# One order of work exchanged for another behind the first batch of a fused attention and feed-forward kernel, with three gates on batch 2's loads

## The chip, the cores and the metric

The kernel runs on one core of a Trainium2 chip. The metric is the device time of one execution in microseconds (us); lower is better. A core has five engines that run their own instruction streams side by side: TensorE (PE) for matrix products, VectorE (DVE), ScalarE (ACT) and GpSimd (POOL) for elementwise work, and SyncE (SP), which here only issues DMA transfers. Each stream runs in order: an instruction that waits holds up everything behind it on its engine.

## What is computed

Linear attention over 8 batches of 8 heads, 576 positions and 64 dimensions, then a feed-forward part with a product of two branches:

```python
q_s = softmax(q, over the head dimension)
k_s = softmax(k, over the positions)
kv = np.einsum('bhsd,bhse->bhde', k_s, v)
x = np.einsum('bhsd,bhde->bhse', q_s, kv)   # then to (4608 tokens, 512)
a = x @ w1                                   # 512 x 1024
b = x @ w2
h = a * b @ w3                               # 1024 x 1024
out = h @ w_out                              # 1024 x 512
```

## The kernel before

The work is cut into steps. Every step has a name, an engine, and the steps that it needs; a table written out by hand, `ORDER`, lists all 977 of them, and `Plan.run` emits them in that order. So the place of a step in the list sets its place in its engine's stream, and a suffix (/A, /D, /P) picks ACT, DVE or POOL where there is a choice. Waits between engines follow from the data and the buffers. Steps marked as `port` on DVE and POOL also wait for the one listed ahead of them on the other of the two.

The number behind a step's name is its batch (0 to 7) or its chunk of 512 tokens (0 to 7, and chunk 8 for the tails of all batches). The steps that matter here, with their lines:

- `q.b`, `k.b`, `v.b`, `w1.i`, `w2.i`: loads (line 354). The weights and batches 0 and 1 are issued from POOL, but for q of batch 0; batches 2 to 7 from SP. `w1.1` is the second half of the columns of w1, 512 KB after its cast to 16 bits; a batch's q, k or v is 1152 KB. q, k and v have two buffers each, used in turn.
- `qmx`, `qsub`, `qexp`, `qsm`, `qeps`, `qrc`, `qn`: softmax of q in two parts per batch: row maximum (DVE, L529), subtraction (L535), exponential (ACT, L543), row sum (DVE, L561), reciprocal (DVE, L572), product (L579). `qd` (SP, L613) turns the result by a DMA transpose.
- `kmx`, `cb`, `ksub`, `kexp`: the same for k over positions: column maximum (DVE, L427), its spread over the partitions (DVE, L451 to L462), subtraction (L466), exponential (ACT, L474). `vc` casts v (L271).
- `kv` (PE, L492) sums k_s times v, `kv2` (DVE, L510 to L513) divides by the sums, `xm` and `xt` (PE, L631) give x, `xs` and `xts` (ACT mostly, L275) copy it out of PSUM.
- `up.1.c.s.u` and `up.0.c.s.u` (PE, L787): x times a block of columns of w2 and of w1; `bs` (ACT, L271) copies the first out, `ab` (DVE, L802) multiplies the two. Chunks 0 and 1 do it in two halves of tokens, s = 0 and 1, with u from 0 to 3; blocks u = 2 and 3 use `w1.1` and `w2.2`.
- `down` (PE, L809) multiplies by w3 @ w_out, which is folded once at the start; `os` copies out, `st` (SP, L836) stores.
- Chunks 5 to 8 form their products by Strassen's scheme with seven products in place of eight: `xd`, `ws`, `um`, `ue`, `uc` going up, and for chunks 4 to 7 `ad`, `wt`, `dm`, `de`, `dc` coming down.

PSUM has eight banks, taken by the PE steps in the listed order and freed by the copies that read them. So a late `ab` holds up the PE step that takes its bank next.

A gate makes a load wait for another load. Before, the first load on SP behind the two early ones (it is `q.2`) waits for the third-last load on POOL (it is `w1.1`); behind `w1.1` POOL issues `q.1.1` and `v.1`:

```python
gate = gates.get(name)
if gate:
    tc.add_manual_dep(st[name].ins, st[gate].ins.name, ..., reason="load order")
...
loads = [n for n in listed if plan.steps.get(n, {}).get("kind") == "load"]
gates[[n for n in loads if plan.steps[n]["eng"] == "SP" and n not in EARLY][0]] = [
    n for n in loads if plan.steps[n]["eng"] == "POOL"][-GATE]
```

Of the kernel before, what the change touches and what calls it, by code (L numbers as in the profile page):

```python
# [121 lines left out]
qsm.6.1 qeps.6.1/A ab.4.0.5 ksub.6.0/P xt.4 xts.4.0/A xts.4.1/A ksub.6.1/P kexp.6.0 qsm.6.0 st.0.3 kv.5 qeps.6.0/A
kv2.5 bs.4.0.6/A qrc.6.0 qn.6.0/P qrc.6.1 down.3.0 os.2.3/A down.3.1 kexp.6.1 qd.5.1 xm.5.0 os.3.0/A xs.5.0.0/A
qmx.7.0 xs.5.0.1/A os.3.1/A qmx.7.1 xm.5.1 xs.5.1.1/A xs.5.1.0/A up.0.4.0.6 up.1.4.0.7 um.5.0.1 ue.5.0.1/A ws.2.1/D
ws.3.0/D um.5.1.1 vc.6.0/A ue.5.1.1/A k.7 wt.4/D ad.4.3/D down.3.2 os.3.2/A xd.5.3/D um.5.1.7 xd.5.1/D xd.5.2/D
ws.4.1/D xd.5.4/D um.5.1.6 um.5.0.6 qn.6.1/P ue.5.1.2/A ue.5.0.2/A ab.4.0.4 ab.4.0.6 um.5.0.7 qd.6.0 ue.5.0.7/A
up.0.4.0.7 um.5.0.2 ue.5.1.7/A bs.4.0.7/A qd.6.1 um.5.1.2 kmx.7.0 qsub.7.1/P qexp.7.1 uc.5.1.1 um.5.0.4 qsub.7.0/P
uc.5.0.3 um.5.0.5 um.5.1.4 ab.4.0.7 down.3.3 uc.5.1.3 os.3.3/A ue.5.0.4/D xt.5 xts.5.1/D ab.5.1.0/P qexp.7.0 xts.5.0/A
kv.6 um.5.1.5 uc.5.0.1 ab.5.0.0/P ue.5.1.4/A uc.5.0.4/P um.5.3.1 ue.5.3.1/A um.5.2.7 kv2.6 ue.5.2.7/A qsm.7.1 xm.6.1
xs.6.1.0/A xm.6.0 st.2.3 um.5.0.3 um.5.3.6 um.5.1.3 um.5.2.1 xs.6.0.1/A xs.6.1.1/D uc.5.1.4/D um.5.3.7 st.3.0  # L130
ue.5.3.2/A um.5.3.5 ad.4.1/D qeps.7.1/A qrc.7.1 ad.4.2/D um.5.2.2 ue.5.2.1/A um.5.2.6 xs.6.0.0/A xd.6.3/P um.5.3.2 v.7
uc.5.2.1 ab.5.1.1 ue.5.3.7/A um.5.3.4 uc.5.3.3 ue.5.3.4/A um.5.2.4 uc.5.3.4/P xd.6.2/P um.6.1.1 ue.5.2.2/A uc.5.2.3
ab.5.2.0/P qsm.7.0 ue.6.1.1/A um.5.2.5 dm.4.7 de.4.7/A ab.5.0.1 uc.5.3.1 qeps.7.0/D dm.4.1 de.4.1/A xd.6.1/D um.6.1.6
ad.4.4/D ue.5.2.4/A qrc.7.0 uc.5.2.4/P um.5.3.3 xt.6 ab.5.3.1 xts.6.1/D um.6.1.7 dm.4.6 dm.4.4 xts.6.0/A xd.6.4/P
kmx.7.1 dm.4.2 um.6.1.2 ue.6.1.2/A dc.4.1 um.5.2.3 vc.7.1/A ab.5.2.1 ue.6.1.7/A um.6.1.4 ab.5.3.0/P de.4.2/A um.6.2.7
st.2.0 uc.6.1.3 st.3.1 qn.7.0/P um.6.1.5 ue.6.1.4/A uc.6.1.4/P dm.4.5 dc.4.3 uc.6.1.1 de.4.4/A um.6.3.7 cb.7 dc.4.4/P
ue.6.2.7/A um.6.0.1 ue.6.3.7/A ue.6.0.1/A ab.6.1.0/D um.6.0.7 ue.6.0.7/A dm.4.3 dc.4.2/A ad.5.3/D um.6.3.1 ksub.7.0/D
ue.6.3.1/A um.6.2.1 ue.6.2.1/A um.6.2.4 ksub.7.1/D um.6.1.3 um.6.3.6 um.6.3.4 dm.5.7 ue.6.3.2/A uc.6.3.3 vc.7.0/A
um.6.2.6 ue.6.2.2/A qn.7.1/P uc.6.2.3 um.6.0.6 ue.6.0.2/A um.6.3.5 ue.6.3.4/D kexp.7.0 um.6.0.4 um.6.2.5 um.6.3.2
uc.6.0.3 uc.6.3.1 um.6.2.2 uc.6.2.1 ab.6.1.1 uc.6.3.4/P um.6.0.5 ue.6.0.4/A uc.6.0.4/P um.6.3.3 ab.6.3.1 dm.5.2  # L140
ad.5.1/D um.6.0.3 dm.5.1 kexp.7.1 kv.7 qd.7.0 ad.5.2/D kv2.7 de.5.7/A ue.6.2.4/A de.5.1/A dm.5.4 dm.5.6 de.5.2/A
ab.6.3.0/P st.4.1 um.6.2.3 dc.5.1 ab.6.0.1 uc.6.2.4/P qd.7.1 xm.7.1 xs.7.1.0/D xm.7.0 ad.5.4/D xs.7.1.1/A dm.5.5
um.7.0.2 xs.7.0.1/A xs.7.0.0/A xd.7.1/D de.5.4/A xd.7.3/D xd.7.2/D st.4.0 xt.7 xd.7.4/P xts.7.1/A xts.7.0/A um.6.0.2
um.7.1.1 dc.5.3 dm.5.3 uc.6.0.1 um.7.0.1 dc.5.2/D ue.7.1.1/A dc.5.4/P ue.7.0.1/A um.7.1.6 ue.7.1.2/D um.7.0.7 um.7.1.2
uc.7.1.1 ab.6.0.0/P ue.7.0.7/A um.7.1.7 ue.7.1.7/A um.7.0.6 ue.7.0.2/A uc.7.0.1 um.7.1.5 um.7.2.1 ab.6.2.1 ue.7.2.1/A
ab.6.2.0/D um.7.3.1 um.7.2.2 uc.7.2.1 um.7.0.5 um.7.1.4 ue.7.1.4/A um.7.0.4 uc.7.1.3 um.7.1.3 uc.7.0.3 st.5.0 um.7.3.2
dm.6.1 um.7.2.6 ue.7.0.4/A ad.6.1/P ad.6.2/D um.7.3.7 uc.7.0.4/D ue.7.3.1/A um.7.3.6 uc.7.3.1 uc.7.1.4/D um.7.2.7
um.7.0.3 ab.7.0.0/D ab.7.1.1 ue.7.2.2/A ad.6.3/D ab.7.1.0/P de.6.1/D ue.7.3.7/A ab.7.0.1 dm.6.2 um.7.2.5 ue.7.3.2/A
um.7.3.5 ue.7.2.7/A dc.6.1 um.7.3.4 dm.6.7 de.6.7/A xd.8.3/P st.5.1 uc.7.3.3 um.7.2.4 uc.7.2.3 dm.6.6 st.3.2
ue.7.2.4/A ue.7.3.4/A uc.7.3.4/D uc.7.2.4/D de.6.2/A xd.8.1/D ad.6.4/D xd.8.2/D dm.6.4 um.8.3.7 um.7.2.3 ue.8.3.7/A  # L150
# [975 lines left out]
```

## Time and profile before

| | |
|---|---|
| time, median of 3 runs | 233.28 us (233.26 to 234.73) |
| the profiled execution: its time, its span | 233.08 us, 231.3 us |
| PE busy | 220.6 us, 95% of the span |
| DVE, ACT, POOL busy | 205.2, 154.0, 155.4 us |
| PE's mean granted clock | 0.997 of full speed |
| moved by DMA | 46.88 MB, mean 203 GB/s |

The profile is one execution, recorded by the hardware. Its span runs from the first to the last instruction; the time of an execution also holds a little around it. A row of a group of instructions gives the line, the engine, the operation, output <- input with shapes, the count, busy time, the mean of one in ns, and the idle time of the engine ahead of them with what ended it. A row in order of time gives start, duration and, in brackets, idle time ahead and its releaser. "SPq" and "POOLq" rows are issues of DMA transfers; a transfer lands some microseconds after its issue.

### The profile page before, as it was taken

To read this page: it belongs to the slowest core of one execution; us is meant where nothing else is said; L and a number is where in the kernel's file an instruction comes from. 1 tells how busy PE (TensorE), PEld (TensorE's weight loads), DVE (VectorE), ACT (ScalarE), POOL (GpSimd) and SP (SyncE) were. 2 spreads that over 40 slices of the span, in tenths; PEclk is the share of its full clock that TensorE was granted. 3 is DMA by queue.
4 is the path that set the end of the run, shared out by engine and by line. 5 is a ranking of instruction groups with operands and counts; after the bars stand their busy time and mean duration, and the time that the engine had idled before them with its cause. 6 is when DMAs were issued, how large, how long until landed. Compare 5 with 4: busy or idle time off the path is not lost.

```text
span 231.3 us, 5574 instructions
## 1 busy us (share of the span) xinstructions
PE 220.6 (95%) x2226; PEld 148.3 (64%) x2226; DVE 205.2 (89%) x346; ACT 154.0 (67%) x254; POOL 155.4 (67%) x105
## 2 busy tenths in 40 slices
...
GB/s 221 215 285 233 308 230 237 388 348 328 203 372 206 350 402 211 270 260 363 265 198 81 294 36 240 150 286 12 12 127 108 44 159 71 4 111 116 3 214 148
DMA packets 38105, 46.88 MB, mean 203 GB/s; under 512 B 18112, under 2 KB 21568, under 8 KB 38080
## 3 DMA queue, kind: packets, MB, share of 16 engines
...
## 4 chain that ended last, share of the span: by engine, by line
PE 72%; DMA 12%; DVE 12%; issue 1%; POOL 1%; ACT 0%; ACTq 0%; POOLq 0%; DVEq 0%
PE pab L787 21%; PE uA L871 12%; DMA w<-in_moe_w_dram 9%; PE po L809 8%; PE dA L911 6%; PE uB L871 6%; DVE km L427 5%; DMA k<-in_k_dram 4%; PE pf L396 3%; PE uC L871 3%; PE dB L911 3%; PE po L824 3%; DVE ab L802 2%; PE pkv L492 2%; PE xm L631 2%; PE dC L911 2%
## 5 line engine op out<-in xcount | busy, mean ns | idle before, releaser
L787 PE MATMUL pab<-x,w2sb 128*128 128x256 f16 (+1 forms) x224 | 40.4, 318 | 0.8 <-ACT x L275 0.8
L787 PE MATMUL pab<-x,w1sb 128*128 128x256 f16 (+1 forms) x224 | 40.2, 318 | 1.0 <-DVE ab L802 1.0
L466 POOL TENSOR_TENSOR k<-k,cb 128x1152 f32<-128x1152 f32 x11 | 28.7, 2629 | 11.8 <-DVE q L535 10.7
L579 POOL TENSOR_TENSOR en<-eq,qr 128x1024 f16<-128x1024 f16 (+1 forms) x14 | 29.7, 2124 | 9.7 <-DVE v L850 4.6
L427 DVE TENSOR_REDUCE km<-k 128x128 f32<-128x1152 f32 x14 | 30.5, 2188 | 3.2 <-DMA k<-in_k_dram 3.2
L787 PEld LDWEIGHTS <-w2sb 128*128 128x128 f16 x224 | 21.5, 98 | 14.6 <-issue 2.2
L787 PEld LDWEIGHTS <-w1sb 128*128 128x128 f16 x224 | 21.8, 98 | 13.9 <-issue 1.6
L809 PE MATMUL po<-W3O,ab 128*128 128x512 f16 x128 | 29.4, 379 | 0.1
L535 POOL TENSOR_TENSOR q<-q,qm 128x1280 f32<-128x1280 f32 (+1 forms) x13 | 27.6, 2143 | 1.0 <-DVE qm L529 1.0
L271 ACT CAST bsb<-pab 128x512 f16<-128x512 f32 x40 | 23.0, 592 | 7.0 <-PE pab L787 6.3
L871 PEld LDWEIGHTS <-w 128*128 128x128 f16 x256 | 24.8, 98 | 3.6 <-issue 0.4
L543 ACT ACTIVATE eq<-q 128x1024 f16<-128x1024 f32 (+2 forms) x16 | 18.7, 1180 | 12.0 <-DVE q L535 9.0
L802 DVE TENSOR_TENSOR ab<-pab,bsb 128x512 f16<-128x512 f32 x40 | 25.7, 670 | 0.1
L529 DVE TENSOR_REDUCE qm<-q 128x16 f32<-128x1024 f32 (+2 forms) x16 | 21.1, 1330 | 4.0 <-DMA q<-in_q_dram 4.0
L561 DVE TENSOR_REDUCE qr<-eq 128x16 f32<-128x1024 f16 (+2 forms) x16 | 21.4, 1338 | 0.0
L809 PEld LDWEIGHTS <-ab 128*128 128x128 f16 x128 | 12.3, 98 | 13.6
L275 ACT ACTIVATE x<-xm 128x512 f16<-128x512 f32 x30 | 16.1, 606 | 6.8 <-PE xm L631 5.9
L474 ACT ACTIVATE ek<-k 128x1152 f16<-128x1152 f32 x16 | 18.4, 1167 | 2.8 <-POOL k L466 2.8
L271 ACT COPY q<-uA 128x512 f32<-128x512 f32 x22 | 13.0, 594 | 8.7 <-PE uA L871 6.9
L871 PE MATMUL uA<-v,w 128*128 128x256 f16 x128 | 18.4, 273 | 0.0
L271 ACT COPY outs<-po 128x512 f32<-128x512 f32 (+1 forms) x19 | 10.7, 568 | 9.2 <-PE po L824 4.5
L396 PE MATMUL pf<-wosb,aux 128*128 128x512 f16 x64 | 15.6, 379 | 0.5 <-DMA wosb<-in_moe_w_out_dram 0.5
...
## 6 DMA issues: line engine op xcount, KB each, us to landing
q<-in_q_dram SPq DMA_DIRECT2D x6, 1152.0 KB, 7.2
k<-in_k_dram SPq DMA_DIRECT2D x6, 1152.0 KB, 9.4
v<-in_v_dram SPq DMA_DIRECT2D x6, 1152.0 KB, 8.1
...
```

Source lines behind the costliest of these rows:

```text
L271: return [(nc.scalar.copy if eng == "ACT" else engine[eng].tensor_copy)(out=out, in_=in_)]
L396: nc.tensor.matmul(st["pf", ft], lhsT=st["w3T", ft][:, gt, :], rhs=wosb[:, gt, :], start=(gt == 0), stop=(gt == N_FT - 1))
L427: dve.tensor_reduce(out=st["km", b][:, two(hp), :], in_=kb[:, two(hp), :, :].rearrange("p h j d -> p h d j"), axis=AX.X, op=ALU.max)
L466: return [engine[eng].tensor_tensor(out=kb[:, two(hp), :, :], in0=kb[:, two(hp), :, :], in1=st["cb", b][:, two(hp), None, :].broadcast_to( ...
L535: return [engine[eng].tensor_tensor(out=qb[:, hs, j, :], in0=qb[:, hs, j, :], in1=st["qm", b][:, hs, j, None].broadcast_to([P, nh, n, D]), ...
L561: dve.tensor_reduce(out=st["qr", b][(slice(None), *part(p))], in_=st["eq", b, p], axis=AX.X, op=ALU.add)
L579: return [engine[eng].tensor_tensor(out=st["en", b][:, j, hs, :].rearrange("p j h d -> p h j d"), in0=st["eq", b, p], in1=st["qr", b][:, h ...
L787: nc.tensor.matmul(st["p", one, c, sub, u][:, a * (t1 - t0):(a + 1) * (t1 - t0)], lhsT=w[:, ct, fb * P:(fb + 1) * P], rhs=x()[:, ct, t0:t1 ...
L802: dve.tensor_tensor(out=st["ab", c][:, nf * u:nf * u + nf, t0:t1], in0=cut(st["p", 0, c, sub, u]), in1=cut(st["bsb", c, sub, u]), op=ALU.mult)
L809: nc.tensor.matmul(st["po", c, tb], lhsT=st["ab", c][:, ft, tb * P:(tb + 1) * P], rhs=W3O[:, ft, :], start=(ft == 0), stop=(ft == N_FT - 1))
L871: nc.tensor.matmul(t[:, u, :], lhsT=w[:, k0 + kk, fb * P:(fb + 1) * P], rhs=r[:, kk, :], start=(p in (1, 2, 7) and u == 0 and kk == 0), st ...
L911: nc.tensor.matmul(t[:, i, :], lhsT=l[:, f, i * P:(i + 1) * P], rhs=r[:, f, :], start=(p in (1, 2, 7) and i == 0 and f == 0), stop=(i == 1 ...
```

## The change

`GATE` and the code that chose the gated load go; a table names the three gated loads and `w1.1` for each of them. `ORDER` is another list of the same 977 steps, equal in the first 140; 56 of the steps that may run on one of two engines run on the other one. Behind `w2.2`, POOL issues `v.1`, `q.1.1`, `w1.1`. Steps, buffers and tiles stay as they are.

```diff
-GATE = 3
+GATES = {(n, 2): ("w1", 1) for n in "qkv"}
...
-up.1.0.1.2 bs.0.1.2/A up.1.0.0.2 up.1.0.0.3 ab.0.0.1 qsm.1.0 qeps.1.0/A qrc.1.0 bs.0.0.3/A bs.0.0.2/A kexp.1.1
-bs.0.1.3/A w1.1 up.0.0.1.2 q.1.1 qmx.1.1 v.1 ksub.1.0/P kexp.1.0 vc.1.1/A up.0.0.0.2 up.0.0.1.3 qn.1.0/P up.0.0.0.3
-ab.0.0.2 ab.0.1.2 ab.0.0.3 down.0.0 down.0.1 ab.0.1.3 q.2 qmx.2.0 qsub.1.1/P qexp.1.1 qsm.1.1 vc.1.0/P kv.1.0 kv.1
-kv2.1 os.0.0/A os.0.1/A qeps.1.1/A qrc.1.1 qmx.2.1 qsub.2.0/P qexp.2.0 qsm.2.0 down.0.2 down.0.3 os.0.2/A k.2 qd.1.0
-q.3 kmx.2.0 v.2 xm.1.0 xs.1.0.0/A xs.1.0.1/A os.0.3/A xt.0 xts.0.1/A ws.1.0/P up.1.1.0.0 up.0.1.0.0 kmx.2.1 up.1.1.0.1
-up.0.1.0.1 qn.1.1/P qd.1.1 bs.1.0.0/A ab.1.0.0 qsub.2.1/P qeps.2.0/A qrc.2.0 qexp.2.1 vc.2.1/A bs.1.0.1/A q.4
-up.1.1.0.2 up.0.1.0.2 xts.0.0/A xm.1.1 xs.1.1.1/A wt.1/P k.3 st.0.0 cb.2 qn.2.0/P qd.2.0 bs.1.0.2/A qsm.2.1 xt.1
-up.1.1.0.3 ab.1.0.1 up.0.1.0.3 ksub.2.1/P xs.1.1.0/A up.1.1.1.0 qeps.2.1/A bs.1.0.3/A xts.1.1/A kexp.2.1 bs.1.1.0/A
-qrc.2.1 qn.2.1/P qd.2.1 qmx.3.1 up.0.1.1.0 up.1.1.1.1 up.0.1.1.1 vc.2.0/A bs.1.1.1/A ab.1.0.3 ksub.2.0/P st.0.2
-ab.1.0.2 qmx.4.0 qmx.3.0 kexp.2.0 kmx.3.0 down.1.0 qmx.4.1 down.1.1 os.1.1/A os.1.0/A kv.2 v.4 up.1.1.1.2 up.0.1.1.2
-xts.1.0/A bs.1.1.2/A kv2.2 xm.2.0 xs.2.0.0/A xs.2.0.1/A xm.2.1 xs.2.1.0/A v.3 kmx.3.1 st.1.0 cb.3 xs.2.1.1/A
-qsub.3.0/P up.1.1.1.3 up.0.1.1.3 up.1.2.0.0 bs.1.1.3/A qsub.3.1/P ab.1.1.3 qexp.3.1 qsm.3.1 k.4 bs.2.0.0/A up.0.2.0.0
-up.1.2.0.1 up.0.2.0.1 qsub.4.1/P qexp.4.1 up.1.2.0.2 up.0.2.0.2 ab.2.0.0 qexp.3.0 q.5 bs.2.0.1/A qeps.3.1/A ab.1.1.0
-qsub.4.0/P qsm.3.0 ksub.3.1/P ksub.3.0/P qrc.3.1 qexp.4.0 ab.1.1.1 up.1.2.0.3 up.0.2.0.3 bs.2.0.3/A ab.1.1.2 qsm.4.1
-up.1.2.0.4 up.0.2.0.4 up.1.2.0.5 qn.3.1/P qeps.3.0/A qrc.3.0 vc.3.1/A kmx.4.0 bs.2.0.4/A ab.2.0.4 down.1.2 qn.3.0/P
-up.0.2.0.5 bs.2.0.2/A kexp.3.0 kexp.3.1 vc.3.0/A kv.3 ab.2.0.1 ws.2.0/P bs.2.0.5/A os.1.2/A qmx.5.0 wt.3/P qd.3.1
-qeps.4.1/A qrc.4.1 qsub.5.0/P xt.2 xts.2.0/A ab.2.0.5 xts.2.1/A down.1.3 os.1.3/A up.1.2.0.6 ab.2.0.2 up.0.2.0.6
-qd.3.0 kv2.3 xm.3.1 xs.3.1.1/A q.6 qn.4.1/P ws.4.0/P xm.3.0 st.1.3 xs.3.0.0/A xs.3.0.1/A kmx.4.1 cb.4 xs.3.1.0/A
-up.1.2.0.7 up.0.2.0.7 bs.2.0.7/A ksub.4.1/P up.1.3.0.0 bs.3.0.0/A v.5 bs.2.0.6/A qexp.5.0 up.0.3.0.0 up.1.3.0.1
-ksub.4.0/P qsm.4.0 qeps.4.0/A ab.2.0.7 st.1.1 qmx.6.1 bs.3.0.1/A up.0.3.0.1 qsm.5.0 up.1.3.0.2 qrc.4.0 qn.4.0/P
-qsub.6.1/P up.0.3.0.2 vc.4.0/A up.1.3.0.3 bs.3.0.2/A up.0.3.0.3 up.1.3.0.4 qd.4.1 bs.3.0.3/A k.5 ab.2.0.6 up.0.3.0.4
-qmx.6.0 ab.2.0.3 qmx.5.1 vc.4.1/A up.1.3.0.5 v.6 up.0.3.0.5 qsub.5.1/P bs.3.0.4/A ab.3.0.4 qsub.6.0/P qd.4.0 down.2.0
-kexp.4.1 wt.2/P kexp.4.0 k.6 down.2.1 ab.3.0.0 st.1.2 st.0.1 vc.5.0/A bs.3.0.5/A kmx.5.0 ab.3.0.3 os.2.0/A kmx.5.1
-xt.3 xts.3.1/A kv.4 kv2.4 qexp.5.1 down.2.2 os.2.1/A xts.3.0/A ws.3.1/P ws.1.1/P ab.3.0.1 xm.4.0 xs.4.0.0/A xs.4.0.1/A
-xm.4.1 xs.4.1.0/A xs.4.1.1/A qsm.5.1 up.1.3.0.6 bs.3.0.6/A up.0.3.0.6 up.1.3.0.7 up.0.3.0.7 st.2.1 qexp.6.1 qeps.5.1/A
-qeps.5.0/A cb.5 ksub.5.1/P ksub.5.0/P ab.3.0.5 up.1.4.0.0 up.0.4.0.0 kmx.6.1 vc.5.1/A bs.3.0.7/A ab.3.0.7 bs.4.0.0/A
...
+up.1.0.1.2 bs.0.1.2/A up.1.0.0.2 up.1.0.0.3 ab.0.0.1 qsm.1.0 qeps.1.0/A qrc.1.0 bs.0.0.3/A bs.0.0.2/A kexp.1.1 v.1
+q.1.1 w1.1 up.0.0.0.2 up.0.0.1.2 qmx.1.1 bs.0.1.3/A ksub.1.0/P up.0.0.0.3 up.0.0.1.3 ab.0.0.2 ab.0.0.3 down.0.0
+ab.0.1.2 down.0.1 ab.0.1.3 qn.1.0/P xt.0 q.2 qmx.2.1 qsub.1.1/P qmx.2.0 kexp.1.0 vc.1.0/A kv.1.0 os.0.0/A qexp.1.1
+vc.1.1/P kv.1 qsm.1.1 qeps.1.1/A kv2.1 qrc.1.1 down.0.2 k.2 qsub.2.1/P qexp.2.1 qd.1.0 xm.1.0 xs.1.0.1/A kmx.2.1
+qsub.2.0/P xs.1.0.0/A down.0.3 qexp.2.0 v.2 qsm.2.1 os.0.2/A os.0.1/A qsm.2.0 q.3 qn.1.1/P qd.1.1 xts.0.1/A up.1.1.0.0
+up.0.1.0.0 qeps.2.1/A vc.2.0/A qrc.2.1 ws.1.0/P k.3 up.1.1.0.1 up.0.1.0.1 qn.2.1/P kmx.2.0 qeps.2.0/A qrc.2.0 cb.2
+qn.2.0/P bs.1.0.0/A bs.1.0.1/A qd.2.0 qmx.3.1 os.0.3/A xts.0.0/A up.1.1.0.2 up.0.1.0.2 up.1.1.0.3 bs.1.0.2/A xm.1.1
+xs.1.1.0/A ab.1.0.2 xs.1.1.1/A up.0.1.0.3 ab.1.0.0 up.1.1.1.0 bs.1.1.0/A ab.1.0.1 bs.1.0.3/A ksub.2.0/P up.0.1.1.0
+kexp.2.0 up.1.1.1.1 bs.1.1.1/A up.0.1.1.1 qmx.3.0 vc.2.1/A q.4 up.1.1.1.2 up.0.1.1.2 kmx.3.1 st.0.0 up.1.1.1.3
+up.0.1.1.3 qd.2.1 bs.1.1.2/A ab.1.1.1 ksub.2.1/P kexp.2.1 v.3 bs.1.1.3/A ab.1.1.2 kv.2 qsub.3.0/P qexp.3.0 k.4
+qsub.3.1/P qexp.3.1 q.5 ab.1.1.0 ab.1.0.3 kv2.2 down.1.0 xm.2.1 xs.2.1.1/A v.4 qmx.4.1 xm.2.0 xs.2.0.0/A xs.2.0.1/A
+down.1.1 xs.2.1.0/A up.1.2.0.0 xt.1 qsm.3.1 qmx.4.0 ws.2.0/P os.1.1/A bs.2.0.0/A qeps.3.1/A up.0.2.0.0 ab.1.1.3
+down.1.2 os.1.2/A xts.1.0/A qsub.4.1/P wt.1/D qrc.3.1 wt.2/D xts.1.1/A up.1.2.0.1 qsub.4.0/P up.0.2.0.1 up.1.2.0.2
+up.0.2.0.2 qsm.3.0 qeps.3.0/A bs.2.0.1/A vc.3.0/A qexp.4.1 qn.3.1/P qd.3.1 kmx.3.0 qrc.3.0 qn.3.0/P bs.2.0.2/A cb.3
+os.1.0/A vc.3.1/A ab.2.0.1 qd.3.0 ab.2.0.0 qexp.4.0 q.6 up.1.2.0.3 up.0.2.0.3 up.1.2.0.4 up.0.2.0.4 v.5 up.1.2.0.5
+bs.2.0.5/A qmx.5.1 ab.2.0.2 up.0.2.0.5 kmx.4.1 ab.2.0.5 bs.2.0.3/A ab.2.0.3 up.1.2.0.6 up.0.2.0.6 up.1.2.0.7 st.1.1
+up.0.2.0.7 ksub.3.0/P kexp.3.0 bs.2.0.4/A st.0.1 bs.2.0.6/A ab.2.0.6 ksub.3.1/P kexp.3.1 qsm.4.0 ab.2.0.4 qeps.4.0/A
+kv.3 kv2.3 bs.2.0.7/A ab.2.0.7 down.1.3 xm.3.1 xs.3.1.0/A xm.3.0 xs.3.0.0/A xt.2 xts.2.1/A st.0.2 xs.3.0.1/A ws.3.0/P
+ws.1.1/P down.2.0 xs.3.1.1/A os.2.0/A up.1.3.0.0 bs.3.0.0/A qsm.4.1 qeps.4.1/A xts.2.0/A up.0.3.0.0 up.1.3.0.1
+up.0.3.0.1 up.1.3.0.2 up.0.3.0.2 kmx.4.0 qsub.5.1/P qexp.5.1 vc.5.0/A bs.3.0.1/A os.1.3/A ws.3.1/P bs.3.0.2/A
+up.1.3.0.3 up.0.3.0.3 up.1.3.0.4 bs.3.0.3/A qrc.4.0 qn.4.0/P vc.4.0/A up.0.3.0.4 up.1.3.0.5 qmx.6.1 qrc.4.1 qn.4.1/P
+bs.3.0.4/A vc.4.1/A cb.4 ksub.4.1/P k.5 qmx.6.0 kexp.4.1 bs.3.0.5/A ksub.4.0/P kexp.4.0 qmx.5.0 qsub.5.0/P st.1.0
+qsm.5.1 down.2.1 ab.3.0.2 ab.3.0.3 ab.3.0.0 os.2.1/A ab.3.0.1 qsub.6.1/P up.0.3.0.5 up.1.3.0.6 bs.3.0.6/A kmx.5.0
+up.0.3.0.6 kv.4 kmx.5.1 ws.4.0/P qexp.5.0 qsm.5.0 xt.3 xts.3.1/A xts.3.0/A vc.5.1/A up.1.3.0.7 st.0.3 up.0.3.0.7
+ab.3.0.5 down.2.2 down.2.3 qexp.6.1 ab.3.0.4 ab.3.0.6 st.1.3 kv2.4 wt.3/P qd.4.0 qd.4.1 bs.3.0.7/A ab.3.0.7 xm.4.1
+qsub.6.0/P os.2.2/A v.6 qeps.5.1/A qrc.5.1 qn.5.1/P xm.4.0 xt.4 xs.4.0.0/A xs.4.1.0/A cb.5 k.6 kmx.6.0 ksub.5.1/P
+qsm.6.1 xs.4.0.1/A down.3.0 down.3.1 xts.4.0/A qexp.6.0 xs.4.1.1/A up.1.4.0.0 bs.4.0.0/A up.0.4.0.0 up.1.4.0.1 kmx.6.1
...
-        loads = [n for n in listed if plan.steps.get(n, {}).get("kind") == "load"]
-        gates[[n for n in loads if plan.steps[n]["eng"] == "SP" and n not in EARLY][0]] = [
-            n for n in loads if plan.steps[n]["eng"] == "POOL"][-GATE]
+        gates.update(GATES)
```

83 lines of the change are left out of this document (41 added, 42 removed).

## The prediction

> **What bounds the kernel now.** I read the page's busy times first, then busy time by stretch, then what TensorE (PE) and the SyncE queue (SP) waited for, then the early stages in order of time.
>
> ```profile
> span 231.3 us, 5574 instructions
> PE 220.6 (95%) x2226; PEld 148.3 (64%) x2226; DVE 205.2 (89%) x346; ACT 154.0 (67%) x254; POOL 155.4 (67%) x105
> ...
> 40.00:50.00 10.00, 10.00 (x83) 7.90 (x81) 8.42 (x11) 7.11 (x10) 7.53 (x4) 1.00 1.05 387
> 50.00:60.00 10.00, 9.16 (x140) 5.79 (x138) 9.86 (x12) 6.06 (x13) 9.02 (x6) 1.00 1.21 318
> 60.00:70.00 10.00, 8.56 (x86) 6.99 (x85) 9.82 (x19) 8.67 (x14) 10.00 (x5) 1.00 0.88 281
> ...
> 90.00:100.00 10.00, 9.80 (x127) 4.54 (x126) 9.72 (x22) 6.79 (x15) 10.00 (x5) 1.00 0.95 245
> ...
> 110.00:120.00 10.00, 8.97 (x122) 4.09 (x120) 9.75 (x19) 6.50 (x14) 10.00 (x6) 1.00 0.95 261
> 120.00:130.00 10.00, 10.00 (x48) 4.56 (x47) 9.85 (x18) 9.03 (x13) 9.16 (x4) 1.00 0.52 150
> ...
> 220.00:231.30 11.30, 7.73 (x56) 4.56 (x53) 3.71 (x7) 2.02 (x4) 1.27 (x1) 0.94 0.58 186
> ```
>
> The columns after the stretch are its length, then busy time of PE, weight loads, VectorE (DVE), ScalarE (ACT), GpSimd (POOL), then PE's granted clock, DMA share and GB/s. PE is the bound: 220.6 of 231.3 us. Both kernels hold the same steps, so PE's own work stays, and only its idle time can move. After 40 us before's PE idles 0.84 us (50 to 60), 1.44 (60 to 70), 0.20 (90 to 100) and 1.03 (110 to 120), together 3.5 us, then nothing until the end. **That 3.5 us is the most that a new order can win behind the first batch.** DVE stands at 9.7 to 9.9 of 10 from 50 us on: the second limit, with no room to catch up.
>
> **The change, part by part.** *The gates.* Before, q.2 at the head of SP waits for w1.1; in after it does too, and the orders of instructions on SP show no wait for w1.1 at k.2 or v.2. They stand behind q.2 in SP's queue, so two of the three listed gates cost and give nothing. What changes is what w1.1 stands behind: POOL issued w2.2, w1.1, q.1.1, v.1; now it is w2.2, v.1, q.1.1, w1.1.
>
> ```profile
> 22.96 0.75 POOL L354 DMA_DIRECT2D q<-in_q_dram  x1 [1.83 <-DMA w<-in_moe_w_dram]
> 23.71 0.75 POOL L354 DMA_DIRECT2D w2sb<-in_moe_w_dram  x1
> 24.82 0.74 POOL L354 DMA_DIRECT2D w1sb<-in_moe_w_dram  x1 [0.36 <-DMA w<-in_moe_w_dram]
> 27.73 0.75 POOL L354 DMA_DIRECT2D q<-in_q_dram  x1 [2.17 <-DMA v<-in_v_dram]
> 30.68 0.75 POOL L354 DMA_DIRECT2D v<-in_v_dram  x1 [2.20 <-DMA k<-in_k_dram]
> ...
> DMA to landing us min/median/max: 15.1/16.3/17.4
> ...
> q<-in_q_dram POOLq DMA_DIRECT2D x1, 640.0 KB, 16.3
> v<-in_v_dram POOLq DMA_DIRECT2D x1, 1152.0 KB, 16.6
> q<-in_q_dram POOLq DMA_DIRECT2D x1, 512.0 KB, 13.8
> w2sb<-in_moe_w_dram POOLq DMA_DIRECT2D x1, 512.0 KB, 15.5
> ...
> 42.34 0.37 SPq L354 DMA_DIRECT2D q<-in_q_dram  x1
> ```
>
> Issue plus time to landing (the row of three figures is w1sb's, its maximum is w1.1) gives q.1.0 36.8, w2.2 39.2, w1.1 42.2, q.1.1 44.0 and v.1 47.3 us: one line, each load some microseconds behind the last, though all were issued by 31 us. q.2 goes 0.1 us after w1.1 lands. Moving w1.1 from first to third of the three leaves their sum, 3.0 + 1.8 + 3.3 = 8.1 us after 39.2, so w1.1 lands by 47.3. Below: w2.2, as big as w1.1, took 2.4 us, not 3.0; at that pace throughout it is 39.2 + 8.1 x 0.8 = 45.7. I take 46.9, near the rows of these very loads, less a little because q.2 no longer runs beside the last one.
>
> The Trainium skill, "DMA: Bandwidth & Descriptors", section "Queues, rings and completion order", says that each DMA engine takes turns between the queues that have work. By that, v.1 shared the engines with q.2 before and alone would have taken half of its 3.3 us, so w1.1 would now land at 45.7. The rows don't bear it out: v.1, beside q.2, moved 1152 KB in 3.3 us, the pace of q.1.1 (640 KB in 1.8) alone.
>
> *PE waits for w1.1.* PE's list is the same up to the w2 halves of chunk 0; the next matmul needs w1.1.
>
> ```profile
> 40.51 3.66 PE L787 MATMUL pab<-x,w2sb 128*128 128x256 f16 x32
> 44.00 3.66 PE L787 MATMUL pab<-x,w1sb 128*128 128x256 f16 x32
> 47.49 3.62 PE L809 MATMUL po<-W3O,ab 128*128 128x512 f16 x16
> 51.04 0.78 PE L492 MATMUL pkv<-v,ek 64*64 64x65 f16 x72
> 51.75 3.63 PE L809 MATMUL po<-W3O,ab 128*128 128x512 f16 x16
> 55.31 0.41 PE L631 MATMUL xm<-qT,kv 64*64 64x256 f16 x8
> 55.55 0.23 PE L631 MATMUL xt<-qT,kv 64*64 64x64 f16 x8
> ...
> 56.40 0.27 PE L787 MATMUL pab<-x,w2sb 128*128 128x256 f16 x1 [0.62 <-ACT x L275]
> ...
> 50.07 1.22 DVE L529 TENSOR_REDUCE qm<-q 128x16 f32<-128x1024 f32 x1 [1.08 <-DMA q<-in_q_dram]
> 51.21 1.48 DVE L561 TENSOR_REDUCE qr<-eq 128x20 f32<-128x1280 f16 x1
> 52.60 0.21 DVE L510 TENSOR_SCALAR rc<-pkv 128x2 f32<-128x2 f32 x2
> ...
> 53.65 1.43 DVE L529 TENSOR_REDUCE qm<-q 128x20 f32<-128x1280 f32 x1
> ```
>
> Before, w1.1 landed 1.8 us ahead of its use at 44.00, so its load was hidden. Landing at 46.9 it is not: **PE stalls 2.9 us** (1.7 to 3.3 by the bounds), and nothing listed ahead can fill it. An up step is a quarter of 40.51 to 44.00, 0.87 us; a down step half of 47.49 to 51.04, 1.77.
>
> *q.2 comes late.* It is issued at 47.0 instead of 42.34. The rows give two bounds for its flight: 50.07 - 42.34 = 7.7 us behind other loads, and 6.2 with little else in flight:
>
> ```profile
> L354 SPq DMA_DIRECT2D q<-in_q_dram x1: 540/540/540, 124.7 to 124.7; - x1
> ...
> DMA to landing us min/median/max: 6.2/6.2/6.2
> ```
>
> I take 6.2, since the line is empty once w1.1 has landed: 53.2 us. DVE's new order puts both row maxima of q.2, then qsm.1.1, ahead of kv2.1, where before had one: 1.43 + 1.14 + 1.39 + 1.05 us by the starts above, so kv2.1 ends at 58.2. PE reaches xm.1.0, which needs it, at 46.9 + 4 x 0.87 + 2 x 1.77 + 0.2 (xt.0) + 0.7 (kv.1) + 1.77 = 56.6: a second stall of 1.6 us. Then xm.1.0 (0.4) and down.0.3 (1.77): the first up step of chunk 1 starts at 60.4, with the same work done as before at 56.40. **The lag is 4.0 us.**
>
> *Chunk 1.* DVE now runs all of batch 2's statistics ahead of the first gate product, ab.1.0.2:
>
> ```profile
> L427 DVE TENSOR_REDUCE km<-k 128x128 f32<-128x1152 f32 x14 | 30.5, 2188 | 3.2 <-DMA k<-in_k_dram 3.2
> ...
> 78.08 0.45 DVE L451 STREAM_TRANSPOSE kmq<-km 128x256 f32<-128x256 f32 x1
> ...
> 80.27 0.65 DVE L802 TENSOR_TENSOR ab<-pab,bsb 128x512 f16<-128x512 f32 x1
> ```
>
> Two kmx at 2.19, cb (78.08 to 80.27) 2.19, qsm 1.39 and 1.14, qmx.3.1 1.43, the product 0.65 and some 0.6 of reciprocals make 11.8 us: it ends at 70.0. PE wants that bank after nine up steps and xm.1.1 (0.56), at 68.8: a stall of 1.2. Before's own stalls in this stretch, 0.22 of the row 50 to 60 and 1.44, don't return. Lag 4.0 + 1.2 - 1.7 = 3.5 at chunk 2.
>
> *Chunks 2 and 3.* Before lost 0.20 + 1.03 here. In after up.0.3.0.7 waits for the bank of ab.3.0.5, which stands on DVE behind kmx.5.0, kmx.5.1 and qsm.5.0 (5.5 us). Between nothing (DVE as full as before) and 2.2 (one kmx more ahead of it than PE has cover for) I take 1.0. Lag 3.5 - 1.2 + 1.0 = 3.3.
>
> *The rest.* Before's PE never waits from 120 to 220 us, so a new order can't win there. What moves between engines (two ksub of batch 6 and two wt onto DVE; additions and products of the Strassen chunks onto POOL) is covered by PE's work as long as DVE keeps up; bounds 0 and +2, the size of one late kmx; I take 0.
>
> **The sum**: 2.9 + 1.6 for the two stalls, less 0.5 for the wait ahead of 56.40 that the second replaces, + 1.2 - 1.7 + 1.0 - 1.2 = 3.3. The profiled execution took 233.08 us (1.8 around its span), 0.2 below the median 233.28. 233.1 + 3.3 = **236.4 us**, 1.3% slower.
>
> **A clock that could fall.**
>
> ```profile
> 227.50:228.00 0.50, 0.23 (x5) 0.05 (x1) 0.23 (x1) 0.00 (x0) 0.00 (x0) 1.00 1.03 406
> ...
> 230.00:230.50 0.50, 0.00 (x0) 0.00 (x0) 0.00 (x0) 0.00 (x0) 0.00 (x0) 0.53 0.01 1
> ```
>
> At the end PE goes idle at 227.7 and its granted clock falls to about half at 230.0, 2.3 us later. A stall of 2.9 us can reach that. If half speed lasts through the four up steps behind it (3.5 us), PE loses up to 3.5 us; 1.6 of it lies under the wait for kv2.1, which hangs on q.2, so +1.9 at most is left. The Trainium skill, "TensorE: Matmul & The Clock Gate", section "Part 1: The HAM clock gate", has the clock halved after an idle window of about 3.4 us, one that runs freely. By that 2.9 us would be safe, and the sum stays 236.4; the row says 2.3 can be enough, depending on where the window lies. I leave it out of the sum and keep it as a rival.
>
> **The rivals.**
> - *The loss is given back* (chance 0.20): w1.1 lands at the lower bound, 45.7, so both late loads come 1.2 us earlier, and DVE has ab.3.0.5 in time. 236.4 - 1.2 - 1.0 = 234.2. For it: w2.2's pace. Against: the three loads' own rows.
> - *Not slower* (0.06): the three loads land in 4.8 us instead of 8.1, by 44.0, PE's next use of w1.1; that is the point from which it decides. Then q.2 is 1.7 us late at most, and the order may save any part of the 3.5 us of idle: 229.6 to 233.1. Against: no neighbouring pair in the line landed at such a pace.
> - *The clock falls* (0.11): 236.4 + 1.9 = 238.3; with q.2 at the 7.7 us flight another 1.5 in place of the cover, 239.2 to 239.8.
> - *New waits in the last chunks* (0.08): one late kmx of 2.19 us that DVE can't make up: 238.6.
> - *The gates do nothing*: true of k.2 and v.2 in any case, at no price; q.2 behind a late w1.1 is not nothing.
>
> **How the numbers follow.** The forecast holds 0.55, from 235.4 to 237.6. About 1% (2.3 us) is what a measurement of this kernel tells from no change. Slower by over 1% (above 235.6): 0.52 of the forecast's chance and both late rivals, 0.71. Faster by over 1%: half of the "not slower" case, 0.03. Within 1%: the rest, 0.26. The range takes in the first rival and the upper end of "not slower" below, and the clock above: 233.3 to 239.4.
>
> **What would show it.** Right: PE idle from 44.0 to about 47 in front of w1sb's matmuls; SP's q.2 issued at 47 instead of 42.3; DVE waiting for q.2 until 53; a second wait of PE ahead of xm.1.0; chunk 1's first up step near 60.4; from 130 us on the same work 3 to 4 us later. Wrong: w1.1 landing at 44 or sooner, PE without a gap at 44, or a lag at chunk 1 that has vanished by chunk 4.

## The result and the profile after

The changed kernel takes **234.88 us** (median of 15 runs, 233.87 to 236.94) against 233.28 (median of 15 runs beside it, 232.61 to 236.78). The ratio is 1.0067, with a 95% interval of 1.0043 to 1.0092: slower by 0.7%, 1.6 us. The forecast was 236.4, 1.3% slower. The time lies in the range, the direction was right, and the loss is half of what was expected. The profiled execution took 234.69 us.

The page of the changed kernel, and its busy time by stretch (the columns as before: length, PE, weight loads, DVE, ACT, POOL, clock, DMA share, GB/s):

```profile
span 232.9 us, 5574 instructions
PE 222.3 (95%) x2226; PEld 148.6 (64%) x2226; DVE 203.9 (88%) x340; ACT 155.5 (67%) x258; POOL 156.7 (67%) x107
...
40.00:50.00 10.00, 7.06 (x54) 5.64 (x52) 6.22 (x8) 6.44 (x9) 7.91 (x4) 0.87 0.76 199
50.00:60.00 10.00, 10.00 (x135) 5.35 (x133) 8.75 (x13) 4.66 (x7) 5.45 (x3) 0.96 1.08 382
...
110.00:120.00 10.00, 8.54 (x116) 4.02 (x115) 9.99 (x13) 8.91 (x13) 10.00 (x5) 1.00 1.01 285
```

The loss stands in one row: from 40 to 50 us PE was idle 2.94 us where before it was never idle, and its clock, full there before, was 0.87. PE's busy time grew by 1.7 us though its matmuls are the same: some of them ran at half clock.

The early stages in order of time, rows of POOL, SP, PE and DVE:

```profile
24.73 0.75 POOL L354 DMA_DIRECT2D v<-in_v_dram  x1 [0.51 <-DMA w<-in_moe_w_dram]
27.65 0.76 POOL L354 DMA_DIRECT2D q<-in_q_dram  x1 [2.17 <-DMA v<-in_v_dram]
30.58 0.75 POOL L354 DMA_DIRECT2D w1sb<-in_moe_w_dram  x1 [2.18 <-DMA k<-in_k_dram]
...
46.71 0.37 SPq L354 DMA_DIRECT2D q<-in_q_dram  x1
47.19 0.44 SPq L354 DMA_DIRECT2D k<-in_k_dram  x1
...
40.09 3.66 PE L785 MATMUL pab<-x,w2sb 128*128 128x256 f16 x32
46.69 5.33 PE L785 MATMUL pab<-x,w1sb 128*128 128x256 f16 x32 [2.94 <-DMA w1sb<-in_moe_w_dram]
...
58.04 0.41 PE L629 MATMUL xm<-qT,kv 64*64 64x256 f16 x8
60.12 1.04 PE L785 MATMUL pab<-x,w2sb 128*128 128x256 f16 x8
...
57.44 0.49 DVE L511 TENSOR_TENSOR kv<-pkv,rc 128x128 f16<-128x128 f32 x2
```

w1.1 is the last of the three loads, PE waits for it until 46.69, and q.2 goes out at 46.71. The four up steps behind the wait take 5.33 us instead of 3.66. After that PE no longer waits: kv2.1 ends at 57.9 and xm.1.0 starts at 58.04.

Where the clock fell, busy time by half microseconds:

```profile
46.50:47.00 0.50, 0.31 (x3) 0.29 (x4) 0.00 (x0) 0.50 (x2) 0.50 (x2) 1.00 0.00 0
47.00:47.50 0.50, 0.50 (x7) 0.42 (x6) 0.00 (x0) 0.50 (x1) 0.50 (x1) 0.93 0.00 0
47.50:48.00 0.50, 0.50 (x5) 0.38 (x3) 0.00 (x0) 0.50 (x2) 0.50 (x1) 0.50 0.88 65
...
50.50:51.00 0.50, 0.50 (x5) 0.39 (x4) 0.00 (x0) 0.00 (x0) 0.00 (x0) 0.66 1.02 406
51.00:51.50 0.50, 0.50 (x7) 0.46 (x5) 0.31 (x1) 0.00 (x0) 0.00 (x0) 1.00 1.04 410
```

The clock drops to half near 47.4, when PE has been at work again for 0.7 us, and returns near 50.8.

The span from 40 us on in four stretches that hold the same PE work in both kernels: from the last w2 steps of chunk 0 to chunk 1's first up step, from there to chunk 4's first, to the last matmul, and to the end. (In before's list three down steps and xt.4 stand behind chunk 4's first up step, at 119.57, that stand ahead of it in the new list; their 5.37 us are counted ahead.) First before, then after:

```profile
40.51:56.40 15.89, 15.27 (x186) 10.35 (x184) 14.17 (x22) 11.27 (x17) 12.95 (x7) 1.00 1.07 352
56.40:124.94 68.54, 65.64 (x609) 35.97 (x609) 64.31 (x101) 53.76 (x89) 67.80 (x31) 1.00 0.94 270
124.94:227.73 102.79, 102.79 (x1072) 79.78 (x1070) 93.81 (x171) 66.46 (x119) 59.48 (x41) 1.00 0.45 120
227.73:231.30 3.57, 0.00 (x0) 0.00 (x0) 0.29 (x1) 0.27 (x1) 0.00 (x0) 0.82 0.36 122
```

```profile
40.09:60.12 20.03, 17.09 (x187) 10.91 (x184) 15.00 (x22) 11.22 (x16) 13.49 (x7) 0.91 0.92 290
60.12:127.21 67.09, 64.84 (x618) 35.52 (x617) 64.56 (x106) 52.12 (x87) 64.67 (x30) 1.00 0.90 266
127.21:230.06 102.85, 102.83 (x1065) 79.83 (x1063) 91.52 (x161) 69.78 (x126) 63.44 (x44) 1.00 0.44 120
230.06:232.90 2.84, 0.00 (x0) 0.00 (x0) 0.29 (x1) 0.00 (x0) 0.00 (x0) 1.00 0.44 149
```

The second column is the length. The differences are **+4.14, -1.45, +0.06 and -0.73**, together +2.02; after's first stretch began 0.42 sooner, which leaves the 1.6 us between the spans. So 4.1 us are lost up to chunk 1's start (the first experiment shows how much of that is the load's), and the new order gives 2.2 back behind it, 0.7 of that at the very end. The 0.4 at the start may belong to the new list too: this block of matmuls starts between 39.70 and 40.21 in ten profiles of kernels with the new list and gates, and between 40.33 and 40.64 in three with the old one; what makes it was not found.

### The profile page after: what moved, and what is told of

Same layout as the page of the kernel before. It is cut to its first block, busy times and chain, and to the rows that moved or that the text cites. A ratio compares the mean times of both kernels' runs of the same rounds, so it can differ in the third digit from the quotient of the medians.

```text
span 232.9 us, 5574 instructions
## 1 busy us (share of the span) xinstructions
PE 222.3 (95%) x2226; PEld 148.6 (64%) x2226; DVE 203.9 (88%) x340; ACT 155.5 (67%) x258; POOL 156.7 (67%) x107
## 4 chain that ended last, share of the span: by engine, by line
PE 63%; DMA 21%; DVE 9%; issue 2%; ACT 2%; POOL 1%; SPq 1%; POOLq 0%; ACTq 0%
PE pab L785 16%; PE uA L869 12%; PE po L807 9%; DMA w1sb<-in_moe_w_dram 7%; DMA k<-in_k_dram 6%; PE dA L909 6%; PE uB L869 6%; DMA w<-in_moe_w_dram 5%; DMA qT<-en 3%; PE uC L869 3%; PE dB L909 3%; PE po L822 3%; DVE km L425 3%; DVE ab L800 2%; PE xm L629 2%
## 5 line engine op out<-in xcount | busy, mean ns | idle before, releaser
L785 PE MATMUL pab<-x,w1sb 128*128 128x256 f16 (+1 forms) x224 | 42.0, 329 | 4.7 <-DMA w1sb<-in_moe_w_dram 2.9
L785 PEld LDWEIGHTS <-w1sb 128*128 128x128 f16 x224 | 22.3, 102 | 18.9 <-DMA w1sb<-in_moe_w_dram 3.2
L464 POOL TENSOR_TENSOR k<-k,cb 128x1152 f32<-128x1152 f32 x9 | 23.5, 2635 | 10.4 <-DVE q L533 10.4
L275 ACT ACTIVATE x<-xm 128x512 f16<-128x512 f32 x31 | 16.7, 605 | 8.1 <-PE xm L629 6.6
L271 ACT COPY q<-uA 128x512 f32<-128x512 f32 x27 | 15.8, 590 | 7.7 <-PE uA L869 5.6
```

The costliest lines, as they stand in the source:

```text
L271: return [(nc.scalar.copy if eng == "ACT" else engine[eng].tensor_copy)(out=out, in_=in_)]
L464: return [engine[eng].tensor_tensor(out=kb[:, two(hp), :, :], in0=kb[:, two(hp), :, :], in1=st["cb", b][:, two(hp), None, :].broadcast_to( ...
L785: nc.tensor.matmul(st["p", one, c, sub, u][:, a * (t1 - t0):(a + 1) * (t1 - t0)], lhsT=w[:, ct, fb * P:(fb + 1) * P], rhs=x()[:, ct, t0:t1 ...
```

## The experiments

Each kernel was timed beside the kernel before, whose medians were 233.6 to 233.7 us in these sets.

### The order without the loads, and the loads without the order

The first has the new list with w1.1 and v.1 in their old places among the loads.

```diff
-kexp.1.1 v.1 q.1.1 w1.1 up.0.0.0.2
+kexp.1.1 w1.1 q.1.1 v.1 up.0.0.0.2
```

> The changed order, but POOL issues w1.1, q.1.1, v.1 as the kernel before did. Theory (the late w1.1 is the loss): w1.1 lands near 42, PE has no gap at 44 and its clock stays at 1.00, q.2 is issued near 42.3 and chunk 1's first up step starts near 57 instead of 60.1, so about 3 us less than the changed kernel: 231.5 to 232.2 us. Rival (the new order itself is slower, DVE gives the early gain back): 233.3 us or more.

Measured: **231.85 us** (231.34 to 233.08), ratio 0.9925 (0.9901 to 0.9950). Rows of PE and DVE, and the four stretches:

```profile
43.47 3.66 PE L785 MATMUL pab<-x,w1sb 128*128 128x256 f16 x32
49.69 2.61 DVE L527 TENSOR_REDUCE qm<-q 128x20 f32<-128x1280 f32 x2 [1.47 <-DMA q<-in_q_dram]
54.42 0.61 PE L629 MATMUL xm<-qT,kv 64*64 64x256 f16 x8 [1.21 <-DVE kv L511]
...
39.98:56.69 16.71, 15.51 (x186) 10.22 (x184) 14.76 (x21) 11.16 (x16) 13.36 (x7) 1.00 1.08 360
56.69:123.95 67.26, 64.86 (x617) 35.58 (x616) 64.61 (x106) 52.19 (x87) 64.81 (x30) 1.00 0.91 270
123.95:226.94 102.99, 102.99 (x1065) 79.94 (x1063) 91.58 (x161) 69.81 (x126) 63.49 (x44) 1.00 0.44 120
226.94:229.80 2.86, 0.00 (x0) 0.00 (x0) 0.29 (x1) 0.00 (x0) 0.00 (x0) 1.00 0.45 153
```

No wait at 43.47 and a full clock. The order alone pays 0.8 us in the first stretch, where the second row maximum of q.2 holds up kv2.1, and 0.2 in the third, and wins 1.3 in the second and 0.7 in the last, much as after does. So of the 4.1 us that after loses in its first stretch 0.8 are the order's and 3.3 the loads' (20.03 against 16.71). The order is good; the loads make the change slower.

The second is the kernel before with the new order of the three loads, and w1.1, now the last, still the one that q.2 waits for.

```diff
-GATE = 3
+GATE = 1
...
-bs.0.1.3/A w1.1 up.0.0.1.2 q.1.1 qmx.1.1 v.1 ksub.1.0/P
+bs.0.1.3/A v.1 q.1.1 w1.1 up.0.0.1.2 qmx.1.1 ksub.1.0/P
```

> The order of before, but POOL issues v.1, q.1.1, w1.1, and q.2 waits for w1.1 as before. Theory: PE idles 2.9 us ahead of the first matmul that needs w1.1, q.2 is issued near 47, and the order of before cannot give this back: 236 to 237 us, 3 to 3.5 us above before. Rival (the late load is harmless in any order, the changed order's own waits are the loss): 233 to 234 us.

Measured: **236.58 us** (234.95 to 237.81), ratio 1.0128 (1.0085 to 1.0171). PE waited as in after, but the clock of this profile stayed full:

```profile
47.18 3.67 PE L787 MATMUL pab<-x,w1sb 128*128 128x256 f16 x32 [2.88 <-DMA w1sb<-in_moe_w_dram]
```

The loads alone cost 1.28%, the order alone wins 0.75%; the product of the two ratios is 1.0052, and both together measured 1.0067. The two parts hardly touch each other.

### No gates

```diff
-GATES = {(n, 2): ("w1", 1) for n in "qkv"}
+GATES = {}
```

> The changed kernel without gates: q.2 and k.2 go as soon as their buffers are free. Theory (queues share the DMA engines, so bytes of q.2 and k.2, 2.36 MB at about 390 GB/s, delay the loads of weights by up to 6 us): w1.1 lands at 50 to 52 and the time is 237 to 239 us. Rival (SP's loads take only bandwidth that POOL's loads leave unused): w1.1 lands near 46.7 as before, q.2 is there long before, and the time is 233.5 to 234.5 us.

Measured: **240.0 us** (238.99 to 242.09), ratio 1.0284 (1.0237 to 1.0332). Batch 2's q and k now run beside the weights:

```profile
33.49 0.37 SPq L354 DMA_DIRECT2D k<-in_k_dram  x1
45.73 3.67 PE L785 MATMUL pab<-x,w2sb 128*128 128x256 f16 x32 [0.47 <-DMA w2sb<-in_moe_w_dram]
52.91 5.33 PE L785 MATMUL pab<-x,w1sb 128*128 128x256 f16 x32 [3.52 <-DMA w1sb<-in_moe_w_dram]
```

w1.1 lands at 52.9 instead of 46.7, 6.2 us later, which is what q.2 and k.2 (2.36 MB together) need at 380 GB/s, the pace of after's row from 50 to 60. So loads on two queues do share the engines. Part of it shows as a later issue: POOL, waiting for its queue, issued w1.1 at 33.98 instead of 30.58. The gate is worth 5.1 us here (240.0 against 234.88, timed in two sets). The 240.0 us are one more than the range expected; the clock also fell further, to means of 0.977 to 0.992 in the six runs.

### The gap filled

Twelve matmuls of zeros that nothing reads stand in after's list ahead of the first step that needs w1.1. They keep PE busy while it would wait.

```diff
-q.1.1 w1.1 up.0.0.0.2
+q.1.1 w1.1 zero.7 up.0.0.0.2
...
-    ZEROS = [13] + [0] * 6
+    ZEROS = [13] + [0] * 6 + [12]
```

> The changed kernel with 12 matmuls of zeros (2.6 us) listed ahead of the first step that needs w1.1; nothing reads them. Theory (the clock's fall is covered by the wait for q.2): the granted clock stays at 1.00, the four up steps take 3.5 instead of 5.2 us, but PE then waits 1.7 us ahead of xm.1.0 for kv2.1, so chunk 1 still starts near 60.1 and the time is the same within 0.5 us, 234.4 to 234.9. Rival (the clock's fall is paid in full): 233.2 us.

Measured: **233.59 us** (233.23 to 234.03), ratio to before 1.0003 (0.9983 to 1.0024).

```profile
43.61 2.75 PE L302 MATMUL zero<-zero 128*128 128x512 f16 x12
46.71 3.67 PE L785 MATMUL pab<-x,w1sb 128*128 128x256 f16 x32 [0.35 <-DMA w1sb<-in_moe_w_dram]
57.05 0.61 PE L629 MATMUL xm<-qT,kv 64*64 64x256 f16 x8 [0.59 <-DVE kv L511]
...
52.32 2.61 DVE L527 TENSOR_REDUCE qm<-q 128x20 f32<-128x1280 f32 x2 [0.89 <-DMA q<-in_q_dram]
```

The load is as late as in after, yet the kernel is 1.3 us faster in the median and its runs lie within 0.8 us instead of 3.1: the four up steps take 3.67 us again, and chunk 1 starts at 59.33 instead of 60.12. The theory that the wait for kv2.1 covers nearly all of the clock's fall was wrong. q.2 landed at 52.3, 5.6 us after its issue, so that wait is only 0.6 us long and covers no more.

After's own runs show what the fall costs, and a remainder. Half clock for 3.4 us takes 0.007 off a run's mean granted clock (an estimate from the rows above). Five runs at 0.999 or more took 233.9 to 234.7 us (median 234.63), six at 0.991 to 0.993, as the profiled one, 233.9 to 235.2 (median 234.91), and four at 0.984 or 0.985 took 235.4 to 236.9. By that estimate one fall costs some 0.3 us in the median and two cost 1.5. The runs at full clock are still 1.0 us slower than the kernel with zeros (233.59), which was timed in another set: that part of its gain isn't explained by the clock, and what makes it was not found. The kernel before has runs at 0.991 to 0.993 too, 8 of the 23 beside this experiment, so a fall isn't peculiar to this wait.

### Two waits taken out of the new order

Both start from the new order with the old loads (231.85). First kv2.1 goes ahead of the second row maximum:

```diff
-q.2 qmx.2.1 qsub.1.1/P qmx.2.0 kexp.1.0
+q.2 qmx.2.1 qsub.1.1/P kexp.1.0
...
-kv2.1 qrc.1.1 down.0.2
+kv2.1 qrc.1.1 qmx.2.0 down.0.2
```

> The new order with the old order of loads, and qmx.2.0 listed behind kv2.1 and qrc.1.1 instead of ahead of them. In the run of the new order with the old loads xm.1.0 waited 1.21 us for kv2.1, and the clock was full. Theory (that wait is on the path and what stands behind kv2.1 on DVE is not): chunk 1 starts about 1.1 us sooner, at 55.6 instead of 56.69, and the time is 230.7 to 231.2 against 231.85. Rival (qmx.2.0 is needed soon by chunk 1's scores, or the gain is waited off at ab.1.0.2): 231.6 to 232.2.

Measured: 232.09 us (231.73 to 233.01), ratio to before 0.9949 (0.9921 to 0.9977); no gain. Then, on top of it, ab.3.0.5 ahead of the two steps in front of it:

```diff
-bs.3.0.6/A kmx.5.0 up.0.3.0.6 kv.4 kmx.5.1
+bs.3.0.6/A kmx.5.0 ab.3.0.5 up.0.3.0.6 kv.4 kmx.5.1
```

> As the kernel with kv2.1 first, and also ab.3.0.5 listed right behind kmx.5.0, ahead of kmx.5.1 and qsm.5.0. In the run of the new order with the old loads up.0.3.0.7 waited 1.44 us for that ab. Theory: the wait goes and nothing takes its place, so 1.2 to 1.4 us less than the kernel with kv2.1 first: 229.3 to 230.0. Rival: kmx.5.1 and qsm.5.0, later by one ab step, hold a later bank, and the time is within 0.4 us of the other kernel.

Measured: 231.81 us (231.42 to 232.67), ratio 0.9942 (0.9916 to 0.9968); no gain either. The rows say where the gains went, two of the first kernel and two of the second:

```profile
53.74 0.41 PE L629 MATMUL xm<-qT,kv 64*64 64x256 f16 x8 [0.29 <-DMA qT<-en]
65.89 1.03 PE L785 MATMUL pab<-x,w1sb 128*128 128x256 f16 x8 [0.86 <-DVE ab L800]
```

```profile
75.74 0.63 PE L629 MATMUL xm<-qT,kv 64*64 64x512 f16 x8 [1.15 <-DMA qT<-en]
116.84 3.61 PE L807 MATMUL po<-W3O,ab 128*128 128x512 f16 x16 [1.37 <-DVE ab L800]
```

xm.1.0 starts 0.7 us sooner, and PE then waits longer at the next gate product (0.86 us instead of 0.41) and 0.28 us at xm.1.1, where it didn't wait before. In the second kernel xm.2.1 waits 1.15 us for its transposed q, 0.47 without the moves. Taking the last ab forward only moves PE's wait of 1.4 us to the down step behind it. That step starts as the first of DVE's next two products ends (they run from 116.10 to 117.39); it doesn't read them, so what it waits for is perhaps a bank, which the rows don't show. Taking either wait away won nothing.

### The end alone

The kernel before, with the last copy on ACT listed ahead of the last one on DVE and of ACT's own store, as in the new list.

```diff
-os.8.2/A os.8.3.0/D down.8.3 st.8.2 st.8.3.0
-os.8.3/D st.8.3 os.8.3.256/A st.8.3.256
+os.8.2/A os.8.3.0/D down.8.3 st.8.2 os.8.3.256/A
+os.8.3/D st.8.3.0 st.8.3.256 st.8.3
```

> The kernel before, with the last steps alone put in the new list's order: os.8.3.256 on ACT ahead of os.8.3 on DVE and of ACT's own store of the last half. Theory (part of the new order's gain is its end, where PE's last matmul stands 2.8 us ahead of the span's end instead of 3.6): 0.7 us less than before, 232.6 to 232.9 against 233.3 to 233.6. Rival (the end is bound by the store's flight, whichever copy goes first): within 0.2 us of before.

Measured: 232.8 us (231.54 to 234.29), ratio 0.9981 (0.9946 to 1.0016). The median is 0.8 us lower, as expected, but the interval doesn't exclude no change. The profile shows the place: before's last copy on ACT, then the same copy here.

```profile
228.09 0.37 ACTq L817 DMA_DIRECT2D out_dram<-outs  x1
228.58 0.27 ACT L271 COPY outs<-po 128x128 f32<-128x128 f32 x1 [1.95 <-DVE outs L271]
```

```profile
226.99 0.27 ACT L271 COPY outs<-po 128x128 f32<-128x128 f32 x1 [0.69 <-DVE outs L271]
```

Before, ACT issued its store, and for that waited for DVE's copy, ahead of its own last copy. Listed the other way, the copy is done first; PE's last matmul ends at 227.4 and the span at 230.3, 2.9 us apart instead of 3.57.

### An earlier gate

The new order with the old loads, and q.2 waiting for w2.1 instead of w1.1.

```diff
-GATES = {(n, 2): ("w1", 1) for n in "qkv"}
+GATES = {(n, 2): ("w2", 2) for n in "qkv"}
```

> The new order with the old order of loads, and q, k and v of batch 2 waiting for the load of w2.1 instead of the last load of weights, so that q.2 is issued near 39.3 instead of 42.3. Theory (queues share the engines, and w1.1 has 1.3 us of slack there, since it lands at 42.2 and is wanted at 43.5): q.2 lands 1.5 to 3 us sooner, w1.1 up to 1.5 us later, xm.1.0's wait of 1.2 us goes at least in part, and the time is 230.8 to 231.6 against 231.85. Rival (the sharing costs w1.1 more than its slack): PE waits for w1.1 by 1 to 2 us at 43.5, and the time is 232.3 to 234.

(The gate is w2.2, the third part of w2, which the expectation calls w2.1; it lands near 39.3.) Measured: 231.98 us (231.42 to 234.51), ratio 0.9952 (0.9916 to 0.9988), the same as with the later gate. PE didn't wait for w1.1, as the theory had it, but q.2 came no sooner, and the time missed both ranges:

```profile
50.32 2.61 DVE L527 TENSOR_REDUCE qm<-q 128x20 f32<-128x1280 f32 x2 [2.03 <-DMA q<-in_q_dram]
55.05 0.60 PE L629 MATMUL xm<-qT,kv 64*64 64x256 f16 x8 [2.12 <-DVE kv L511]
```

q.2 landed at 50.3, issued 2.4 us earlier (39.55 against 41.93), against 49.7. The DMA moved some 390 GB/s from 41 to 50 us with either gate: what is sent earlier shares the engines with what is still under way.

### Does DVE set the pace behind q.2?

In the four profiles of the new order with the old loads above DVE is busy some 9.7 of 10 us from 52 to 110 us. The more it idles there (1.5, 1.6, 1.9 and 2.0 us), the longer is the span (229.8, 230.0, 230.3 and 231.0 us), though the medians don't follow. So work was added to DVE, and some was moved out of the stretch. Three copies of output blocks went from ACT to DVE in that stretch:

```diff
-os.0.3/A  ...  os.1.1/A  ...  os.2.0/A
+os.0.3/D  ...  os.1.1/D  ...  os.2.0/D
```

> The new order with the old order of loads, and three copies of output blocks in the stretch from 56 to 112 us (os.0.3, os.1.1, os.2.0) on DVE instead of ACT. A copy of half that size takes DVE 0.42 us, so each is some 0.7 us there. Theory (from the load of q.2 to PE's wait for DVE at 115 it is DVE that sets the pace: in seven runs the span follows DVE's idle time in that stretch): 2.1 us of work more on DVE are 1.7 to 2.1 us more of time, 233.5 to 234.0 against 231.85. Rival (PE sets the pace there, and DVE's work beside it costs nothing but a wait here and there): 231.6 to 232.5.

Measured: **234.43 us** (233.88 to 234.98), ratio to before 1.0032 (1.0007 to 1.0056), 2.6 more than without. Then one copy in the gap ahead of qmx.2.1:

```diff
-q.2 qmx.2.1 ... kv.1.0 os.0.0/A qexp.1.1
+q.2 os.0.0/D qmx.2.1 ... kv.1.0 qexp.1.1
```

> The new order with the old order of loads, and one such copy (os.0.0) on DVE instead of ACT, listed right ahead of qmx.2.1, where DVE sits idle for 1.47 us until q.2 lands. Theory (DVE's idle time there is free): 0.7 us of work more on DVE cost nothing, 231.6 to 232.2 against 231.85. Rival (any work added to DVE costs its length): 232.4 to 232.7.

Measured: **231.59 us** (231.21 to 232.07), ratio to before 0.9913 (0.9883 to 0.9944). In the gap the copy is free. Then two of the three copies, with the third left on ACT:

```diff
-os.0.3/A  ...  os.1.1/A
+os.0.3/D  ...  os.1.1/D
```

> The new order with the old order of loads, and two of the three copies (os.0.3, os.1.1) on DVE instead of ACT; the third, ahead of which DVE waited 2.7 us for PE, stays on ACT. Theory (DVE sets the pace): 2 x 0.68 = 1.4 us more, 233.0 to 233.4 against 231.85, so that the third one with its wait was worth another 1.2. Rival (the three copies' loss came from that wait alone): 231.7 to 232.2.

Measured: 232.43 us (232.26 to 233.23), ratio 0.9961 (0.9940 to 0.9983): 0.6 more for 1.4 us of work. The third copy was the dear one, since in the first of these kernels DVE stood 2.7 us in front of it:

```profile
99.91 0.69 DVE L271 COPY outs<-po 128x512 f32<-128x512 f32 x1 [2.72 <-PE pab L785]
```

Last, 1.3 us of DVE's work (wt.1 and wt.2) moved out of the stretch:

```diff
-qsub.4.1/P wt.1/D qrc.3.1 wt.2/D xts.1.1/A
+qsub.4.1/P qrc.3.1 xts.1.1/A
...
-qeps.5.1/A qrc.5.1 qn.5.1/P
+qeps.5.1/A wt.1/D wt.2/D qrc.5.1 qn.5.1/P
```

> As the kernel with one copy in DVE's gap, and also wt.1 and wt.2 (0.68 and 0.63 us on DVE, with 0.36 of idle time between) listed ahead of qrc.5.1 near 119 us, where DVE waits 1.0 us in any case, instead of near 78 us. Theory (DVE sets the pace from q.2's landing to PE's wait of 1.4 us for ab.3.0.5 at 115): that wait gets shorter by 1.0 to 1.4 us and the time is 230.2 to 230.7 against 231.6. Rival (PE sets the pace, or the gain is lost to a wait elsewhere, as when the wait for kv2.1 or for ab.3.0.5 was taken away): 231.3 to 232.0.

Measured: 232.43 us (232.25 to 233.72), ratio 0.9965 (0.9940 to 0.9990), 0.8 slower than without the move, timed in another set. In the place of the work that left, DVE waits for ACT (1.17 us instead of 0.36 in the first row, and 0.74 that weren't there before), and PE's wait at the end of the stretch stayed (1.60 us for 1.43):

```profile
79.45 0.28 DVE L570 RECIPROCAL qr<-qr 128x20 f32<-128x20 f32 x1 [1.17 <-ACT qr L565]
92.41 0.69 DVE L800 TENSOR_TENSOR ab<-pab,bsb 128x512 f16<-128x512 f32 x1 [0.74 <-ACT bsb L271]
115.70 1.02 PE L785 MATMUL pab<-x,w1sb 128*128 128x512 f16 x4 [1.60 <-DVE ab L800]
```

So the theory that DVE alone sets the pace fell. Work added to it behind q.2's landing cost 0.4 of its length with two copies and more than its length with three; the work moved out gained nothing. These rows have DVE waiting for PE and for ACT, and PE for DVE, so it looks as if the three stand in one chain there; no run shows that by itself. Which list would be shorter in this stretch stays open.

## Why the prediction was half right

- **The gates.** Right: SP waits for w1.1 once, at q.2, and k.2 and v.2 go out behind it without a wait of their own.
- **w1.1's landing and PE's wait.** Right, 46.7 and 2.94 us for 46.9 and 2.9. Working out the landing from the line of loads served well; by issue and landing v.1 took 3.3 us, q.1.1 1.7 and w1.1 2.4 of the 3.0 that it took before. The sentence that the rows don't bear out that queues take turns held for v.1, which took 3.3 us without q.2 beside it as it had with it. Its comparison was weak, since q.2 had been issued at 42.34 and q.1.1, from 42.2 to 44.0, was hardly alone. And without gates, two loads of batch 2 on SP's queue put w1.1 off by 6.2 us, so loads on two queues do share the engines. The Trainium skill, "DMA: Bandwidth & Descriptors", section "Queues, rings and completion order", agrees with that run, which doesn't show the turns themselves. Still, the landing that I worked out from its rule (45.7) was a microsecond too early.
- **The clock.** The step that left its fall out of the sum failed. It fell in the profiled run and added 1.67 us to the four up steps. Against the trace with the gap filled the first stretch is 0.8 us longer (20.03 against 59.33 - 40.12 = 19.21). The cover was taken as 1.6 us because q.2's flight was taken as 6.2; it was 5.6, and the wait behind it 0.6. Over the runs one fall costs some 0.3 us in the median, two 1.5. The Trainium skill, "TensorE: Matmul & The Clock Gate", section "Part 1: The HAM clock gate", gives a window of 3.4 us that runs freely. Half clock from about 47.4 to 50.8 is that long, and the window ahead of it, 44.0 to 47.4, was idle but for its last 0.7 us. I had read the Trainium skill as making 2.9 us of idle time safe; the row decides that it isn't. A like wait, 2.88 us, left the clock full in the profile of the old order with the new loads.
- **The lag at chunk 1.** 60.12 for 60.4, by a sum of other terms, and that the sizes agree is luck. 2.94 + 1.67, less some 0.5 of before's own wait, gives 4.1, where the prediction had 2.9 + 1.6 - 0.5 = 4.0. The clock stood in the place of the second wait.
- **Chunks 1 to 3.** Mis-sized: -1.45 for -0.7. Of that, PE's idle time is -0.65 (2.25 for 2.90 us), as the sum had it, but by two terms whose errors nearly cancel. The wait for ab.1.0.2's bank was 0.34 for 1.2 us and that for ab.3.0.5 was 1.46 for 1.0, together 1.8:

```profile
PE pab L785 <- DVE ab L800: 1.8, 2, 1.5
```

  The columns are the total, the number of times, and the longest of PE's waits for DVE's products. The other 0.8 us is a term that was not seen: before spends that much more than after here in time that counts as busy (65.64 against 64.84 for the same work). What makes it was not found.
- **The rest.** The step "I take 0" failed, and with it the bound of 3.5 us on what an order can win, which counted PE's idle time alone. PE doesn't wait from 120 us on, but its last matmul isn't the end: the copies and stores behind it took 2.84 us for 3.57. That is -0.73. The 0.4 us at the start wasn't foreseen either.
- **The rivals.** The time came out next to "the loss is given back" (234.2), yet not by its way: w1.1 didn't land at 45.7, and ab.3.0.5 was not in time. "The clock falls" happened in ten of the 15 runs by their mean granted clock, but cost less than its 1.9 us. "Not slower" and "new waits in the last chunks" didn't happen.

In one line: the lag at chunk 1 came out as sized, 4.1 us for 4.0, partly by luck, and what the order gives back behind it, 2.2 us, was left out but for 0.7.

The best versions are the new order with the old loads, 231.85 us, and the same with one copy in DVE's gap, 231.59: 0.8 and 0.9% faster than before.
